# Last transposes in two bank pairs and last output in two column halves, in a fused RWKV-7 and SoLU kernel

## Chip, cores and metric

The kernel runs on one core of a Trainium2 chip. The metric is device time in microseconds (us), the median of several runs. The engines of the core run side by side, each through its own queue in program order, and meet by semaphores: PE (matrix products and transposes), DVE (vector), ACT (scalar and activations), POOL (GpSimd; it also issues DMAs) and SP (SyncE; it issues DMAs only). Products land in PSUM. This kernel treats PSUM as four pairs of banks named A, B, C and h, each 128 partitions by 2 x 512 fp32 values.

## The reference

An RWKV-7 attention over 4 batches, 8 heads, 768 steps and 40 values a head, whose output, as a matrix of 3072 tokens by 320, goes through a SoLU block of width 1024:

```python
for t in range(S):
    y[:, :, t] = np.einsum('bhd,bhde->bhe', rt, state)
    Sa = np.einsum('bhde,bhe->bhd', state, at)
    state_decay = state * wt[:, :, None, :] - np.einsum('bhd,bhe->bhde', Sa, bt)
    state = state_decay + np.einsum('bhd,bhe->bhde', vt, kt)
...
h = x @ w_in
h_max = np.max(h, axis=-1, keepdims=True)
e = np.exp(h - h_max)
sm = e / (np.sum(e, axis=-1, keepdims=True) + 1e-09)
solu = h * sm
mu = np.mean(solu, axis=-1, keepdims=True)
var = np.mean((solu - mu) ** 2, axis=-1, keepdims=True)
ln = (solu - mu) / np.sqrt(var + 1e-06) * g_ln
return (ln @ w_out).astype(np.float32)
```

The gain g_ln and the subtraction of the mean are folded into the output weights (`w2`), and the division by the root of the variance is applied last, row by row (`rs`).

## The kernel before

The work is cut into N = 24 chunks: 12 stretches of 64 time steps for each of two pairs of batches. A chunk is 128 rows (two batches by 64 steps). One loop, `for i in range(-1, N + LAG + 1)` with LAG = 2 (L943), holds a software pipeline. In iteration i the attention works at chunk i (and prepares i + 1 to i + 5), the SoLU block's first product and its softmax work at chunk c = i - 2, and the transposes and the second product work at chunk c - 1 = i - 3. From i = 24 on there is no attention left; i = 25 holds the softmax of chunk 23, the last, and i = 26 only the transposes and output of chunk 23. The order on each engine is the order in which the program emits the instructions.

The steps of the SoLU block, with their lines:

- `hidden` (L741 and on; products recorded at L285, tile `h`): x times w_in, in five pieces of the contraction, into pair h. `left` (L733) issues the loads of xT for it on SP (L739), from the DRAM tile x_dram that `leave` writes by three POOL DMAs (L729 to L731).
- `highest` (L762, DVE, nmax), `exped` (L770, ACT, e), `weighed` (L778, DVE: e becomes h times e, and its mean mu).
- `spreadof` (L781): ACT computes the sum of squares `sq` (L791), whose full-size result is thrown away into a PSUM pair, then `var` (L792); POOL raises it to the power -0.5, `rs` (L793).
- `folded` (L795): sixteen PE transposes (L804) of e, two for each of the eight features (a feature is 128 of the 1024 columns), into one pair, `plnT`. One ACT copy (L809), emitted somewhat later, brings all of it into the SBUF tile lnT.
- `output` (L814): for each of the eight features two products 160 columns wide (`in_parts`, recorded at L285, tile `po`); each shows as two passes in the trace, so a chunk has 32. Then `stored`: ACT multiplies by rs into `osb` (L828) and two DMAs of 64 rows by 320 columns write the output (L831), both on SP except for chunk 23, whose second one goes by ACT's queue. In the steady iterations two of the eight features are held back to the next iteration (the list `rest`); chunk 22's `stored` alone is held back in `late`.

In the last iterations the pairs are used so. `turn` names B and C in alternation as X and Y. The products of `hidden` go to h. The transposes go to h up to chunk 20 and to turn["Y"] for chunks 21 to 23 (`last`, L800). `sq` goes to h, and to A for chunks 22 and 23 (L791). The products `pyo` of `read` (L685) go to A; `summed` (L699, DVE) reads them, and `finish`, what it returns, is `leave`, which makes x and issues the x_dram DMAs. In iteration 26 the order on PE is: the transposes of chunk 23, then chunk 23's products; those of chunk 22 came whole in iteration 25.

Of the kernel before, what the change touches and what calls it, by code (L numbers as in the profile page):

```python
# [9 lines left out]
FP32 = mybir.dt.float32  # L10
# [3 lines left out]
AF = mybir.ActivationFunctionType  # L14
# [3 lines left out]
P = 128  # L18
C = 64
Q = 32  # L20
GRP = 2
AHEAD = 5
LANDS_NEXT = {2: 6, 3: 7, 4: 8, 5: 11, 6: 9, 7: 10, 8: 12}
LAG = 2
EARLY = 10
NK = 5
FIRST = 6
# [26 lines left out]
def kernel(  # L54
# [18 lines left out]
    nc = tc.nc  # L73
    B, H, S, D = r.shape
    DM = H * D
    DFF = moe_w_in.shape[1]
    NCH = S // C
    NPAIR = B // 2
    N = NPAIR * NCH
    NF = DFF // P  # L80
# [5 lines left out]
    two = ctx.enter_context(tc.tile_pool(name="two", bufs=2))  # L86
# [12 lines left out]
    def c_(name):  # L99
        lo, hi = where[name]  # L100
        return cst[:, lo:hi]

    ident, tri = c_("ident"), c_("tri")
# [20 lines left out]
    for x in ex_t:  # L124
# [10 lines left out]
                          in_=c_("eye_hi").unsqueeze(1).to_broadcast([P, 8, Q]))  # L135
# [5 lines left out]
    w2 = const.tile([P, NF, DM], FP32, name="w2")  # L141
# [3 lines left out]
    def pair(tag, name):  # L145
        return psum.tile([P, 2, 512], FP32, tag=tag, name=name)

    turn = dict(X="B", Y="C")
# [119 lines left out]
    def half(p):  # L268
        return slice(C * p, C * p + C)
# [14 lines left out]
    def mm(o, lhsT, rhs, start=True, stop=True):  # L284
        nc.tensor.matmul(o, lhsT=lhsT, rhs=rhs, start=start, stop=stop, skip_group_check=True)  # L285
# [3 lines left out]
    def in_parts(o, lhsT, rhs, start, stop, n=2):  # L289
        width = rhs.shape[-1] // n  # L290
        for x in range(n):
            part = slice(width * x, width * x + width)
            mm(o[:, part], lhsT, rhs[:, part], start and not x, stop)
# [8 lines left out]
    st = [dict() for _ in range(N + 16)]  # L302
    blocks, inverse = {}, {}

    def where_(i):
        return i % NPAIR, i // NPAIR
# [7 lines left out]
    def ok(i):  # L314
        return 0 <= i < N
# [33 lines left out]
    def logged(i):  # L349
        lw = st[i]["lw"] = two.tile([P, DM], FP32, tag="lw", name="lw", bufs=1)  # L350
        nc.scalar.activation(out=lw, in_=st[i]["raw_w"].rearrange("p h d -> p (h d)"), func=AF.Ln)  # L351
# [61 lines left out]
    def decay_turned(i, t=None, y=0):  # L413

        if not ok(i):
            return lambda: None
        ex = st[i]["ex"] = ex_t[i % (AHEAD + 2)]
        t = turned(pair("B", "pei") if t is None else t, y, ei_t[0])
        return lambda: nc.scalar.copy(out=ex[0:W2, :, :, 1:], in_=t)

    def front(i, t=None, y=0):
        if not ok(i):
            return lambda: None
        d = st[i]
        t = turned(pair("C", "pa") if t is None else t, y, d["raw_a"])
        aT = d["aT"] = tokens("aT", AHEAD)
        return lambda: nc.vector.tensor_tensor(out=aT[0:W2], in0=t, in1=d["ex"][0:W2, :, :, 0:C], op=ALU.mult)
# [157 lines left out]
    def attend_r(i, t, y):  # L585
        if not ok(i):
            return lambda: None
        t = turned(t, y, r_t[0])

        def evict():  # L590
            st[i]["rT"] = kept("rT", t)
        return evict
# [179 lines left out]
    def weighed(i):  # L772

        if not ok(i):
            return
        d = st[i]
        d["mu"] = small.tile([P, 1], FP32, tag="mu", name="mu")
        nc.vector.scalar_tensor_tensor(out=d["e"], in0=d["h"], scalar=1.0 / DFF, in1=d["e"], op0=ALU.mult, op1=ALU.mult,  # L778
                                       accum_out=d["mu"])

    def spreadof(i):  # L781

        if not ok(i):
            return
        d = st[i]
        c2 = small.tile([P, 1], FP32, tag="c2", name="c2")
        sq = small.tile([P, 1], FP32, tag="sq", name="sq")
        var = small.tile([P, 1], FP32, tag="var", name="var")
        rs = d["rs"] = small.tile([P, 1], FP32, tag="rs", name="rs")
        nc.scalar.activation(out=c2, in_=d["esum"], func=AF.Square, scale=1e-3 / DFF, bias=guard)  # L790
        nc.scalar.activation(out=pair("A" if i > N - LAG - 1 else "h", "sq").rearrange("p a b -> p (a b)"), in_=d["e"], func=AF.Square, scale=-float(DFF), bias=d["mu"], accum_out=sq)  # L791
        nc.scalar.activation(out=var, in_=sq, func=AF.Identity, scale=1.0 / DFF ** 3, bias=c2)  # L792
        nc.gpsimd.tensor_tensor(out=rs, in0=var, in1=mhalf, op=ALU.pow)  # L793

    def folded(i):  # L795
        if not ok(i):
            return lambda: None
        d = st[i]
        lnT = d["lnT"] = two.tile([P, NF, P], FP32, tag="lnT", name="lnT", bufs=1)
        last = i > N - LAG - 2  # L800
        t = pair(turn["Y"] if last else "h", "plnT")
        for f in range(NF):
            for p in range(2):
                nc.tensor.transpose(out=t[:, p, f * C:f * C + C], in_=d["e"][half(p), f * P:(f + 1) * P],  # L804
                                    identity=ident[half(p), half(p)])

        def evict():
            o, y = lnT.rearrange("q f (p t) -> q p f t", p=2), t.rearrange("q p (f t) -> q p f t", f=NF)
            nc.scalar.copy(out=o, in_=y)  # L809
        return evict  # L810

    late, rest = [], []

    def output(i, t, first=NF):  # L814
        if not ok(i):
            return
        d = st[i]
        bp, ci = where_(i)
        t = t[:, 0:DM]

        def products(lo, hi):
            for f in range(lo, hi):
                in_parts(t, d["lnT"][:, f, :], w2[:, f, :], f == 0, f == NF - 1)
        products(0, first)

        def stored():
            osb = two.tile([P, DM], FP32, tag="osb", name="osb", bufs=1)
            nc.scalar.mul(out=osb, in_=t, mul=d["rs"])  # L828
            for p in range(2):
                queue = nc.scalar if i == N - 1 and p else nc.sync  # L830
                queue.dma_start(out=out.rearrange("(b s) n -> b s n", b=B)[2 * bp + p, ci * C:ci * C + C], in_=osb[half(p)])  # L831
        if first < NF:
            rest.append((lambda: products(first, NF), stored))
        elif i == N - 2:
            late.append(stored)
        else:
            stored()

# [104 lines left out]
    for i in range(-1, N + LAG + 1):  # L943
        j, c = i + AHEAD, i - LAG
# [17 lines left out]
        if i < EARLY - AHEAD:  # L962
            tc_, ta = pair("C", "pa"), pair("A", "pb")
            front_out, r_out = front(j, ta, 0), attend_r(i + 1, ta, 1)
            fold_out = folded(c - 1)
            ei_out, b_out = decay_turned(j + 1, tc_, 0), front_b(j, tc_, 1)
            kv_out = attend_kv(i + 1, pair(turn["X"], "pkv"))
            r_out()
            front_out()
            if i < EARLY - AHEAD:  # L970
                vector(plan[0])
                fold_out()
                b_out()
            else:
                b_out()
                vector(plan[0])
                fold_out()
            s_out = stated(i + 1, pair("A", "pst"), 0) if ok(i + 1) else lambda: None
            for evict in (ei_out, kv_out, s_out):
                evict()  # L980
        else:
            turn.update(zip("XY", ("BC", "CB")[(i - EARLY + AHEAD) % 2]))
            ta = pair("A", "pa")
            front_out, b_out = front(j, ta, 0), front_b(j, ta, 1)
            kv_out = attend_kv(i + 1, pair(turn["Y"], "pkv"))
            front_out()
            kv_out()
            b_out()
            for products, stored in rest:
                products()  # L990
                stored()
            rest.clear()
            vector(plan[0])
            fold_out = folded(c - 1)
            ts = pair("A", "pst")
            s_out = stated(i + 1, ts, 0) if ok(i + 1) else lambda: None
            tc_ = pair(turn["X"], "pb")
            r_out, ei_out = attend_r(i + 1, tc_, 0), decay_turned(j + 1, tc_, 1)
            if i == EARLY - AHEAD and ok(j + 2):
                logged(j + 2)  # L1000
            cum_out = decay_by_halves(j + 2, ts)
            for evict in (r_out, ei_out, fold_out, s_out, *late):
                evict()
            late.clear()
# [65 lines left out]
        finish = summed(i)  # L1070
# [3 lines left out]
            decay(j + 2, pair("C", "pcum")[:, 0])()  # L1074
        tb = pair(turn["X" if i < EARLY - AHEAD else "Y"], "po")
        weighed(c)
        spreadof(c)
        if i >= 0:
            some(Q, (i + 2) // GRP)
# [5 lines left out]
            if odd:  # L1085
                load_keys(j + 3, "k")
                load_keys(j + 5, "w")
        finish()
        vector(plan[5])
        output(c - 1, tb[:, 0], FIRST if EARLY - AHEAD <= i < N - 1 else NF)  # L1090
        if i == -1:
            turn_g(tb[:, 0])
        if i == LAG - 1:
# [33 lines left out]
```

## Time and profile before

| what | value |
|---|---|
| median of 3 runs | 542.85 us (542.31 to 543.46) |
| profiled execution, its own time | 546.59 us |
| its span, first to last instruction | 544.4 us |
| PE busy | 485.0 us, 89% |
| DVE, ACT, POOL busy | 427.4 (79%), 314.4 (58%), 221.0 (41%) us |
| mean granted PE clock | 0.975 |
| HBM read and written | 47.96 and 14.16 MB |

The span is cut by the page into 40 slices of 13.6 us, each digit the busy share in tenths. In the last three slices PE stands at 9, 9 and 6 and DVE at 3, 2 and 0. The stretch that the change touches runs from 501.7 us (the transposes of chunk 20) to the end. In it the trace has the SoLU blocks of chunks 21, 22 and 23, one after the other, each some 9.6 us, the attention of chunk 23 in the first 10 us, and then the last output. Idle time of an engine costs something only where the chain of waits, followed back from the last instruction, goes through it.

### The profile page before, as it was taken

To read this page: it belongs to the slowest core of one execution; us is meant where nothing else is said; L and a number is where in the kernel's file an instruction comes from. 1 tells how busy PE (TensorE), PEld (TensorE's weight loads), DVE (VectorE), ACT (ScalarE), POOL (GpSimd) and SP (SyncE) were. 2 spreads that over 40 slices of the span, in tenths; PEclk is the share of its full clock that TensorE was granted. 3 is DMA by queue.
4 is the path that set the end of the run, shared out by engine and by line. 5 is a ranking of instruction groups with operands and counts; after the bars stand their busy time and mean duration, and the time that the engine had idled before them with its cause. 6 is when DMAs were issued, how large, how long until landed. Compare 5 with 4: busy or idle time off the path is not lost.

```text
span 544.4 us, 28043 instructions
## 1 busy us (share of the span) xinstructions
PE 485.0 (89%) x12029; PEld 397.4 (73%) x12029; DVE 427.4 (79%) x1753; ACT 314.4 (58%) x626; POOL 221.0 (41%) x368
## 2 busy tenths in 40 slices
PE   4634665888999999999999999999999999999996
PEld 3523565756878878878887888788778877787765
DVE  4595998999988987997987979979979798443320
ACT  4733466568467666656665765665556655665333
POOL 4544546244253534536354363545444421211100
PEclk9999975699999999999999999999999999999999
DMA  8998878766455666666684676576563552411210
GB/s 144 160 144 154 191 134 199 159 139 136 74 125 115 114 126 126 138 131 117 132 153 104 115 149 126 114 136 120 113 123 97 108 117 56 104 44 30 54 55 24
DMA packets 198155, 63.95 MB, mean 117 GB/s; under 512 B 170904, under 2 KB 190336, under 8 KB 198032
## 3 DMA queue, kind: packets, MB, share of 16 engines
q1 hardware_dynamic: 185296, 42.22, 42.7%
q0 software_dynamic: 10384, 19.30, 14.7%
q8 instruction: 94, 1.54, 1.2%
q10 hardware_dynamic: 2352, 0.66, 0.7%
q14 instruction: 29, 0.24, 0.2%
HBM read 47.96 MB, written 14.16 MB: 114 GB/s over the span
## 4 chain that ended last, share of the span: by engine, by line
PE 72%; DVE 11%; ACT 7%; DMA 5%; issue 2%; SPq 2%; POOL 0%; ACTq 0%; POOLq 0%; DVEq 0%
PE po L285 19%; PE h L285 18%; PE px L285 6%; PE pyo L285 6%; PE py L285 5%; PE ps L285 3%; PE pu L285 3%; DVE prod L516 2%; DVE uu L519 2%; PE plnT L804 2%; PE pb L400 2%; PE psr L285 2%; DMA raw_w<-in_w_dram 2%; PE pa L400 2%; PE pkv L400 1%
## 5 line engine op out<-in xcount | busy, mean ns | idle before, releaser
L285 PE MATMUL h<-w_in,xT 64*64 64x512 f32 (+1 forms) x1064 | 122.2, 551 | 1.1 <-ACT lnT L809 1.1
L285 PE MATMUL po<-w,lnT 128*128 128x160 f32 x768 | 115.1, 304 | 1.2 <-ACT lnT L809 1.2
L285 PEld LDWEIGHTS po<-w,lnT 128*128 128x128 f32 x768 | 105.4, 190 | 5.8 <-ACT lnT L809 1.3
L519 DVE TENSOR_TENSOR uu<-uu,prod 128x48 f32<-128x48 f32 (+19 forms) x576 | 105.7, 223 | 0.0
L516 DVE TENSOR_TENSOR prod<-blk,uu 128x48 f32<-128x48 f32 (+19 forms) x576 | 102.9, 218 | 1.4
L483 POOL DMA_DIRECT2D nt_dram<-nt x86 | 51.0, 599 | 81.2 <-ACT nt L475 80.0
L793 POOL TENSOR_TENSOR rs<-var,mhalf 128x1 f32<-128x1 f32 x24 | 18.2, 757 | 148.4 <-ACT var L792 148.4
L762 DVE TENSOR_REDUCE nmax<-h 128x1 f32<-128x1024 f32 x24 | 29.3, 1219 | 31.9 <-PE h L285 31.9
L285 PEld LDWEIGHTS h<-w_in,xT 64*64 64x64 f32 x1064 | 38.3, 133 | 19.6 <-issue 14.8
L791 ACT ACTIVATE sq<-e,mu 128x1024 f32<-128x1024 f32 x24 | 26.9, 1119 | 24.2 <-DVE e L778 24.2
L770 ACT ACTIVATE e<-h,nmax 128x1024 f32<-128x1024 f32 x24 | 26.7, 1111 | 21.0 <-DVE nmax L762 21.0
L444 DVE TENSOR_TENSOR lu<-pu,cst 128x512 f32<-128x512 f32 x24 | 16.5, 686 | 25.9 <-PE pu L285 25.6
L311 POOL DMA_DIRECT2D raw_r<-in_r_dram x48 | 33.3, 699 | 0.6 <-issue 0.6
L558 ACT ACTIVATE wy<-py,cst 128x256 f32<-128x256 f32 x24 | 11.4, 474 | 38.1 <-PE py L285 38.1
L508 DVE SCALAR_TENSOR_TENSOR uu<-blk,uu 128x30 f32<-128x30 f32 (+3 forms) x144 | 29.1, 254 | 3.8 <-DMA blk<-nt_dram 3.2
L778 DVE SCALAR_TENSOR_TENSOR e<-h,e 128x1024 f32<-128x1024 f32 x24 | 29.2, 1216 | 3.6 <-ACT e L770 3.4
L393 POOL TENSOR_TENSOR kb<-raw_b,inv 128x320 f32<-128x320 f32 x24 | 21.1, 878 | 26.5 <-DMA raw_b<-in_b_dram 19.1
L617 ACT COPY st<-psr 128x416 f32<-128x416 f32 (+1 forms) x44 | 14.2, 375 | 29.4 <-PE psr L285 29.4
L285 PEld LDWEIGHTS py<-tu,nt 64*64 64x64 f32 x768 | 17.8, 145 | 17.2 <-issue 12.0
L285 PE MATMUL pcum<-lw,cst 128*128 128x160 f32 x48 | 15.3, 465 | 15.9 <-ACT lw L351 15.9
L285 PEld LDWEIGHTS py<-aT,bT 40*64 40x64 f32 x768 | 17.8, 155 | 15.7 <-issue 8.1
L664 ACT ACTIVATE x<-px 128x832 f32<-128x832 f32 x24 | 20.7, 864 | 11.0 <-PE px L285 11.0
(146 smaller groups left out, 1107.1 us busy)
## 6 DMA issues: line engine op xcount, KB each, us to landing
xT<-x_dram SPq DMA_DIRECT2D x48, 160.0 KB
blk<-nt_dram POOLq DMA_DIRECT2D x22, 256.0 KB, 4.1
raw_w<-in_w_dram SPq DMA_DIRECT2D x48, 80.0 KB
a<-in_a_dram SPq DMA_DIRECT2D x48, 80.0 KB
raw_r<-in_r_dram POOLq DMA_DIRECT2D x48, 80.0 KB, 4.3
lv<-in_v_dram SPq DMA_DIRECT2D x48, 80.0 KB
out_dram<-osb SPq DMA_DIRECT2D x47, 80.0 KB
raw_b<-in_b_dram SPq DMA_DIRECT2D x44, 80.0 KB
```

Of the source, the lines that this page charges most:

```text
L285: nc.tensor.matmul(o, lhsT=lhsT, rhs=rhs, start=start, stop=stop, skip_group_check=True)
L311: queue.dma_start(out=x[half(p), :, 0:D], in_=ap[2 * bp + p, :, ci * C:(ci + 1) * C, :].rearrange("h t d -> t h d"))
L393: nc.gpsimd.tensor_tensor(out=kb[:, j:j + H, 0:D], in0=d["raw_" + n], in1=heads(d["inv"]), op=ALU.mult)
L400: nc.tensor.transpose(out=t[0:W2, p, at + C * j:at + C * j + C], in_=x[half(p), 2 * j:2 * j + 2].rearrange("p a b -> p (a b)")[:, skip:ski ...
L483: queue.dma_start(out=blocks[n][e].rearrange("(a x h) s c -> a x s h c", a=GRP, x=2)[at, x], in_=nt[home:home + Q].rearrange("p h j c -> p ...
L508: nc.vector.scalar_tensor_tensor(out=u[:, c, j + 1:Q], in0=nb[:, j, j + 1:Q], scalar=u[:, c, j:j + 1], in1=u[:, c, j + 1:Q], op0=ALU.mult, ...
L516: nc.vector.tensor_tensor(out=ts[-1], in0=nb[:, j:j + 1, j + 1:Q].to_broadcast([P, hi - lo, m]), in1=u[:, lo:hi, j:j + 1].to_broadcast([P, ...
L519: nc.vector.tensor_tensor(out=u[:, lo:hi, j + 1:Q], in0=u[:, lo:hi, j + 1:Q], in1=x, op=ALU.add)
L762: nc.vector.tensor_reduce(out=nmax, in_=d["h"], axis=AX.X, op=ALU.max, negate=True)
L770: nc.scalar.activation(out=e, in_=d["h"], func=AF.Exp, bias=d["nmax"], accum_out=d["esum"])
L778: nc.vector.scalar_tensor_tensor(out=d["e"], in0=d["h"], scalar=1.0 / DFF, in1=d["e"], op0=ALU.mult, op1=ALU.mult, accum_out=d["mu"])
L791: nc.scalar.activation(out=pair("A" if i > N - LAG - 1 else "h", "sq").rearrange("p a b -> p (a b)"), in_=d["e"], func=AF.Square, scale=-f ...
```

## The change

Chunk 20's transposes go to pair A in place of h. In iteration 23 `finish()` is emitted ahead of `spreadof`. One feature of chunk 22's output is held back and emitted behind the transposes of chunk 23; chunk 22's eviction stays in `late`, behind the copies of lnT. Chunk 23's transposes go to two pairs, four features in turn["Y"] and four in A, copied out by DVE and ACT into two tiles. Chunk 23's `sq` goes to h. Its output is computed 160 columns at a time into two pairs, h and turn["Y"], each with an eviction and two stores of 64 rows by 160 columns; the fourth store goes by ACT's queue.

```diff
-        nc.scalar.activation(out=pair("A" if i > N - LAG - 1 else "h", "sq").rearrange("p a b -> p (a b)"), in_=d["e"], func=AF.Square, scale=-float(DFF), bias=d["mu"], accum_out=sq)
+        nc.scalar.activation(out=pair("A" if i == N - 2 else "h", "sq").rearrange("p a b -> p (a b)"), in_=d["e"], func=AF.Square, scale=-float(DFF), bias=d["mu"], accum_out=sq)
...
+        if i == N - 1:
+            return folded_last(d)
         lnT = d["lnT"] = two.tile([P, NF, P], FP32, tag="lnT", name="lnT", bufs=1)
-        last = i > N - LAG - 2
-        t = pair(turn["Y"] if last else "h", "plnT")
+        t = pair("h" if i < N - LAG - 2 else "A" if i == N - LAG - 2 else turn["Y"], "plnT")
...
+    def folded_last(d):
+        n = NF // 2
+        d["lnT"] = (two.tile([P, 2 * n, P], FP32, tag="kvT", name="lnT", bufs=1),
+                    two.tile([P, 2 * n, P], FP32, tag="lnT", name="lnT", bufs=1))
+        ts = pair(turn["Y"], "plnT"), pair("A", "plnT")
+        for f in range(NF):
+            for p in range(2):
+                nc.tensor.transpose(out=ts[f // n][:, p, f % n * C:f % n * C + C],
+                                    in_=d["e"][half(p), f * P:(f + 1) * P], identity=ident[half(p), half(p)])
+
+        def evict():
+            for copy, lnT, t in zip((nc.vector.tensor_copy, nc.scalar.copy), d["lnT"], ts):
+                copy(out=lnT[:, 0:n].rearrange("q f (p t) -> q p f t", p=2),
+                     in_=t[:, :, 0:n * C].rearrange("q p (f t) -> q p f t", f=n))
+        return evict
+
+    def output_last(i):
+        d = st[i]
+        bp, ci = where_(i)
+        n, width = NF // 2, DM // 2
+        for x, tag in enumerate(("h", turn["Y"])):
+            cols = slice(width * x, width * x + width)
+            t = pair(tag, "po")[:, 0, 0:width]
+            for f in range(NF):
+                mm(t, d["lnT"][f // n][:, f % n, :], w2[:, f, cols], f == 0, f == NF - 1)
+            osb = two.tile([P, 4 * P], FP32, tag=("s", "x")[x], name="osb", bufs=1)[:, 0:width]
+            nc.scalar.mul(out=osb, in_=t, mul=d["rs"])
+            for p in range(2):
+                queue = nc.scalar if x and p else nc.sync
+                queue.dma_start(out=out.rearrange("(b s) n -> b s n", b=B)[2 * bp + p, ci * C:ci * C + C, cols], in_=osb[half(p)])
...
-                queue = nc.scalar if i == N - 1 and p else nc.sync
-                queue.dma_start(out=out.rearrange("(b s) n -> b s n", b=B)[2 * bp + p, ci * C:ci * C + C], in_=osb[half(p)])
+                nc.sync.dma_start(out=out.rearrange("(b s) n -> b s n", b=B)[2 * bp + p, ci * C:ci * C + C], in_=osb[half(p)])
...
-        elif i == N - 2:
-            late.append(stored)
...
+            if i == N + LAG:
+                fold_out = folded(c - 1)
             for products, stored in rest:
                 products()
-                stored()
+                if i == N + LAG:
+                    late.append(stored)
+                else:
+                    stored()
             rest.clear()
             vector(plan[0])
-            fold_out = folded(c - 1)
+            if i < N + LAG:
+                fold_out = folded(c - 1)
...
         weighed(c)
+        if i == N - 1:
+            finish()
         spreadof(c)
...
-        finish()
+        if i != N - 1:
+            finish()
         vector(plan[5])
-        output(c - 1, tb[:, 0], FIRST if EARLY - AHEAD <= i < N - 1 else NF)
+        if i == N + LAG:
+            output_last(c - 1)
+        else:
+            output(c - 1, tb[:, 0], NF - 1 if i == N + LAG - 1 else FIRST if EARLY - AHEAD <= i < N - 1 else NF)
```

## The prediction

> **What bounds the kernel now.** First the page's busy shares: PE 89%, DVE 79%, ACT 58%, and the granted clock 0.975. Only the end of the program is edited: the order of instructions on every engine is the same up to chunk 20's transposes, so I read the chain of waits there. Its columns are start and length in us, then what ran.
>
> ```profile
> 497.25 4.54 PE po L285 x32
> 501.80 0.66 PE plnT L804 x16
> 502.45 0.02 issue
> 502.48 1.02 ACT lnT L809
> 503.50 0.04 issue
> 503.54 1.09 PE h L285 x8
> ...
> 525.04 4.53 PE h L285 x40
> 529.57 0.02 issue
> 529.60 1.24 DVE nmax L762
> ...
> 533.36 1.25 ACT sq L791 x2
> 534.61 0.02 issue
> 534.63 0.14 ACT var L792
> 534.77 0.06 issue
> 534.83 1.00 ACT lnT L809
> 535.84 0.04 issue
> 535.88 4.63 PE po L285 x32
> ...
> 540.66 0.53 ACT osb L828
> ```
>
> From 502 on PE sets the end, except in two places. At 502.45 it has finished the transposes of chunk 20 and stands until ACT has copied them out at 503.50, because chunk 21's first product goes to the pair h that still holds them. At 529.57 the last softmax begins (nmax, exp, e, sq, var, then the copy lnT, one after the other), and chunk 23's products start at 535.88. The waits of the same stretch price both stops (total, times, longest, in us):
>
> ```profile
> PE po L285 <- ACT lnT L809: 1.2, 1, 1.2
> PE h L285 <- ACT lnT L809: 1.1, 1, 1.1
> ```
>
> After the last product come one eviction, two stores side by side, and SyncE's wait for them:
>
> ```profile
> 541.22 0.54 ACTq L831 DMA_DIRECT2D out_dram<-osb  x1
> ```
>
> ```profile
> SPq L1122 <- DMA out_dram<-osb: 1.4, 1, 1.4
> ```
>
> **The change, part by part.** Times are on the clock of before; the first part moves all later ones alike.
>
> *Chunk 20's transposes in pair A.* The h products of chunk 21 no longer wait for L809. They could start when the sixteen transposes end, 502.45, as they do in the next chunk, where plnT runs 514.75 to 515.39 and h starts at 515.39. Gain 503.54 - 502.45 = 1.09. What else they need is there: sq of chunk 20, which also writes h, ends at 501.11 (its accumulator read, 500.92 + 0.19), and xT of chunk 21 was issued at 488.65; the loads issued at 507.34 and 519.14 had their last packets at 510.56 and 522.09, some 3 us later. Pair A is free: its last reader, the sum tot, began at 497.32 and took 1.09. The new wait falls on pyo of chunk 23, which takes A after the copy ends at 503.50; PE comes to it at 506.88 - 1.09 = 505.79, with 2.3 us to spare. Behind it on PE are the rest of h and everything after.
> Does the lead last? Each later step (h, nmax, exp, e, transposes) hangs on PE's own products, so they move together. The one input that does not move is xT of chunk 22, landed at 510.56 and needed at 515.33 - 1.09 = 514.24. I take the whole 1.09; the ends are 0 and 1.12.
>
> *finish() ahead of spreadof at i = 23.* On POOL the three x_dram issues (L729 to L731: 0.69 + 0.58 + 0.54 = 1.8 us) now stand before rs of chunk 21, which waited for var. They start when x is ready (L725: 513.24 + 0.76 = 514.00) and not at 515.63. ACT and DVE order are unchanged. xT of chunk 23 then lands 1.6 us earlier relative to PE; its last packet came at 522.09 and it was needed at 524.97, and the whole chain moves together, so 2.9 us of room grow and are worth nothing. SP keeps its order, so its next issue, the store of chunk 20, waits as before for ACT. rs of chunk 21 ends near 514.00 + 1.8 + 0.56 = 516.4 and its reader, osb of chunk 21, ran at 525.19: hidden by 8.8 us. Cost 0; without that cover 0.8 (516.4 against 515.63).
>
> *One feature of chunk 22 behind the last transposes.* Chunk 22's 16 products (32 passes) run 529.43 to 533.97, 4.54 / 32 = 0.142 us a pass; e of chunk 23 is ready at 533.32. With 28 passes first, PE is free at 529.43 + 28 x 0.142 = 533.40, and after a wake-up of about 0.05 (lnT's copy ends 535.82, the weight load starts 535.88) the transposes start at 533.45, not 533.97. They take 0.64, to 534.09, and the four passes left 0.57, to 534.66.
>
> *Two bank pairs, DVE and ACT.* The eighth transpose ends at 533.45 + 0.32, with 0.07 of drain (h issues end 529.50, its chain piece 529.57); DVE starts at 533.87. A DVE copy of 128x512 is not in the trace; the 104x512 copy bT L440 took 0.68, the 128x512 product L444 0.69. So it ends at 534.55, and PE may read it at 534.61: just before PE is done with chunk 22. ACT waits for the last feature of chunk 22 (a signal stands there in the built program, none at the sixteenth transpose), which costs nothing, since var holds ACT until 534.83; behind that copy on ACT stand chunk 22's osb and the last two. Its half takes 0.59 (rT L410, 104x512), to 535.42; PE needs it after eight passes, 534.66 + 1.14 = 535.80. So chunk 23's products start at 534.66 and not at 535.88: gain 1.22. Ends: 0.95 if the DVE copy costs as much as ACT's whole one (1.00), 1.28 if no wake-up costs anything. Chunk 22's osb slips behind the copy, its rs is ready at 525.98, and its store ends far ahead of the last one.
>
> *The last output by 160 columns.* The same 32 passes of the same width run in another order: 0. The first half's osb and stores lie under the second half's 2.27 us of products: products done at 536.93, osb to 537.4, SP's two issues to 538.5; chunk 22's two, ahead of them on SP, end near 537.1, and the last store comes at 539.9, so nothing on SP holds it. Of the last osb, 160 columns go: copies of 416 and 96 columns took 505 and 244 ns (L617), so 0.82 ns a column, 0.13 (ends 0 and 0.33, the latter from 196 ns for 8 columns, L243). PE's end now stands as a wait on the activation itself, where 540.51 to 540.66 held a separate wait: 0.05, ends 0 and 0.11.
> The stores halve. The last two were issued at 541.21; the packets, 1280 bytes each, ran 542.34 to 543.13 one transfer behind the other, and completion was seen at 543.49. A 1280-byte packet took 55 ns, a 512-byte one 27 (xT), so 640 bytes should take about 32: 0.79 x (1 - 32/55) = 0.33 at best, 0 if issue sets the pace. I take 0.25, since the two transfers followed without a gap. The Trainium skill, "DMA: Bandwidth & Descriptors", section "Anatomy of one DMA", gives about 2.0 us fixed for a transfer and the rest by bytes at 436 GB/s, fitted on another issue path; by that the 80 KB less are worth an estimated 0.19, and the sum would be 0.06 smaller. The 2.28 us from issue to completion, of which packets are 0.79, agree with a mostly fixed price.
> A loss stands behind it. SyncE ends with a row of semaphore waits, about 0.062 apart (541.78, 541.84, 541.90, ...). In before the last stores hold lanes six and seven, so one wait followed the one that ended at 543.49; now they hold lanes zero and one at the row's head, and seven follow: +6 x 0.062 = 0.37 (ends 0 and 0.37).
>
> **Sum.** -1.09 - 1.22 - 0.13 - 0.05 - 0.25 + 0.37 = -2.37. On the profiled execution: span 544.4 to 542.0; its own time, 546.59, would be 544.2. The runs' median is 542.85, 3.74 below that profiled run; the tail's waits are the same in both, so 542.85 - 2.37 = 540.5. Unknown terms at their ends, the first held at 1.09: -1.67 to -3.14, so 539.7 to 541.2 for the likeliest case.
>
> **Rivals.**
> 1. The two halves are not really apart: DVE's copy is released only with the last signal, behind chunk 22's feature. It would start at 534.66 + 0.10, end at 535.44, and products start at 535.50: 0.84 lost, total -1.53, 541.3. For it: ACT's half is released just so. Against: the eighth transpose carries a signal of its own in the built program. 8%.
> 2. The 1.09 is given back: pyo of chunk 23 or xT of chunk 22 is what PE then waits for. Total -1.28, 541.6. For: two waits are added at A. Against: 2.3 and 3.7 us of room. 6%.
> 3. Little moves, because what the first 500 us vary by from run to run covers it, or both stops return elsewhere: about 542.4, between 0 and -1.09. For: the three runs span 1.15 us. Against: not one instruction there is reordered. 8%.
> 4. Slower: a PE without its two rests loses clock. The page's row of granted clock shows that this can happen:
>
> ```profile
> PEclk9999975699999999999999999999999999999999
> ```
>
> Slices six to eight stand at 7, 5 and 6. PE's 37 us from 503 to 540 at a share x take 37 (1/x - 1) more; against the 2.37 that decides from x = 0.94, and at 0.88 costs 5.0, so 545.5. Against: 32 slices of nine follow, at PE busy 9, and the rests are 1.1 and 1.2 us. 3%.
>
> **How the numbers follow.** Forecast 75%, the rivals 8, 6, 8 and 3. The predicted time is 540.5. A measurement of this kernel can tell about 0.2%, 1.09 us, from no change. Rivals 1 and most of 2 count as faster: 0.75 + 0.08 + 0.04 = 0.87. Same 0.10, slower 0.03. The range takes in the likeliest's 539.7 to 541.2, rivals 1 and 2, and 0.3 of run-to-run scatter below: 539.4 to 541.9. That leaves out rivals 3 and 4 and little else.
>
> **What would show it.** In the changed profile: h of chunk 21 starts with no wait for lnT; pyo of chunk 23 doesn't wait; the last transposes start within 0.1 us of e's end; DVE's lnT copy takes about 0.68 and ends as the last four passes of chunk 22 do; PE then runs on without a gap until the last osb of some 0.40; from the last issue to the end of the span it is 3.2 us plus or minus 0.3. It is wrong if PE waits over 0.3 us for either half of lnT, if a new wait shows between 503 and 529, or if the last stores' packets take as long as before.

## The result and the profile after

| | before | changed |
|---|---|---|
| median | 543.02 us (11 runs, 542.31 to 544.17) | 540.13 us (11 runs, 538.11 to 542.55) |
| profiled execution: time, span | 546.59, 544.4 | 538.5, 536.7 |
| chunk 20's transposes begin at | 501.72 | 496.35 |
| from there to the end of the span (the tail) | 42.72 | 40.37 |

The ratio of the times is 0.9941, 95% interval 0.9924 to 0.9957: the kernel became 2.3 to 4.1 us faster, against 2.37 forecast. The two profiles differ by 7.7 us, and most of that is not the change. The changed kernel's profile is already 5.37 us ahead where the first changed instruction stands. A tail counted from that point takes this out: 42.72 - 40.37 = 2.35. A run's time is also longer than its span, by 2.14 us in the profiled execution of before and by 1.78 in that of the changed kernel; this difference is taken up at the end of the section on the prediction.

The chain of waits of the changed kernel, start and length in us:

```profile
491.88 4.54 PE po L285 x32
496.42 0.64 PE plnT L805 x16
497.07 1.02 PE h L285 x8
...
522.96 4.00 PE po L285 x28
526.96 0.64 PE plnT L820 x16
527.60 5.23 PE po L285 x36
532.83 0.02 issue
532.86 0.39 ACT osb L839
```

Both stops of before, at 502.45 and at 529.57 on its clock, are gone. After chunk 20's transposes PE goes straight to h, and the last softmax (nmax, exp, e, sq, var) is no longer on the chain: it lies beside the 28 passes of chunk 22. From there to the last product the chain stays on PE: 28 passes, 16 transposes and 36 passes, with one short wait of 0.1 us for DVE's copy inside the 36. The timeline shows how the two copies meet it (start, length, engine, what; in brackets the idle time before and what ended it):

```profile
526.89 0.57 PEld L820 LDWEIGHTS plnT<-cst,e 64*128 64x128 f32 x16 [0.17 <-DVE e L778]
527.40 0.69 DVE L825 COPY lnT<-plnT 128x512 f32<-128x512 f32 x1 [0.61 <-PE plnT L820]
527.53 5.05 PEld L285 LDWEIGHTS po<-w,lnT 128*128 128x128 f32 x36
...
528.38 0.58 ACT L825 COPY lnT<-plnT 128x512 f32<-128x512 f32 x1
```

DVE's copy starts while PE is still at the second eight transposes, so it has its own signal. It ends at 528.09, and chunk 23's products begin at 528.20. ACT's copy ends at 528.96, ahead of their need after eight passes. SyncE's wait for the last stores, which was 1.4 us in before:

```profile
SPq L1163 <- DMA out_dram<-osb: 1.6, 1, 1.6
```

It is longer although the stores are half as large, since it now begins at the head of SyncE's closing row of semaphore waits.

### The profile page after: what moved, and what is told of

Same layout as the page of the kernel before. It is cut to its first block, busy times and chain, and to the rows that moved or that the text cites. A ratio compares the mean times of both kernels' runs of the same rounds, so it can differ in the third digit from the quotient of the medians.

```text
span 536.7 us, 28054 instructions
## 1 busy us (share of the span) xinstructions
PE 480.9 (90%) x12029; PEld 393.6 (73%) x12029; DVE 427.2 (80%) x1754; ACT 314.3 (59%) x627; POOL 222.1 (41%) x368
## 4 chain that ended last, share of the span: by engine, by line
PE 72%; DVE 9%; ACT 6%; DMA 5%; SPq 4%; issue 2%; POOL 1%; ACTq 0%; DVEq 0%; POOLq 0%
PE po L285 20%; PE h L285 18%; PE px L285 5%; PE pyo L285 5%; PE py L285 5%; PE ps L285 3%; PE pu L285 3%; DMA uu_dram<-uu 2%; PE plnT L805 2%; SPq L311 2%; PE pb L400 2%; PE psr L285 2%; PE pa L400 2%; DVE prod L516 2%; DVE uu L519 2%
## 5 line engine op out<-in xcount | busy, mean ns | idle before, releaser
L516 DVE TENSOR_TENSOR prod<-blk,uu 128x48 f32<-128x48 f32 (+19 forms) x576 | 104.5, 221 | 1.4
```

The source lines that it names most:

```text
L516: nc.vector.tensor_tensor(out=ts[-1], in0=nb[:, j:j + 1, j + 1:Q].to_broadcast([P, hi - lo, m]), in1=u[:, lo:hi, j:j + 1].to_broadcast([P, ...
```

## The experiments

All tails are counted from the first weight load of chunk 20's transposes, which every kernel has at the same place in its order of instructions.

**e0_before_again**: the kernel before, without an edit.

> The kernel before, unaltered, profiled once more. The tail is measured from the first weight load of chunk 20's transposes to the end of the span: 42.73 us in the first profile of before (501.72 to 544.45), 40.37 in the changed kernel (496.35 to 536.72). Theory (the whole effect lies in the tail, and the 5.37 us by which the changed kernel's profile is ahead when the tail begins are scatter between executions): tail 42.7 within 0.1, while the start of the tail moves by some us from 501.7. Rival (the changed kernel also gains before the tail): the tail starts near 501.7 again, within 1 us.

Measured: tail 42.73, begun at 501.03. The tail repeats to 0.01 us, as both theories have it; the start moved by 0.7 only, which is the rival's number. One more execution was too few. Over all profiles of this study the tail begins at 501.72 and 501.03 (before), 498.56 (e1), and at 496.35, 500.60, 500.26, 498.10, 501.88, 502.99, 498.50, 496.93 and 497.63 (the changed kernel, e2 to e9). The same instructions in the same order stand ahead of that point in all twelve. Kernels with the changed end lie on both sides of before's, 6.6 us apart among themselves. The runs were made on several chips (e0 to e3 on chip 4, e4 to e7 on chip 6, e8 and e9 on chip 10), but the chip alone does not explain it: e4 to e7 begin 4.9 us apart on one chip, and before's own spans in 17 runs on that chip go from 540.1 to 547.4. So the 5.37 between the first two profiles is within the scatter of executions.

**e1_pair_a_only**: before, with chunk 20's transposes in A.

```diff
-        t = pair(turn["Y"] if last else "h", "plnT")
+        t = pair(turn["Y"] if last else "A" if i == N - LAG - 2 else "h", "plnT")
```

> The kernel before with one part alone: chunk 20's transposes go to pair A. Theory: PE no longer stands before chunk 21's first product, and the lead lasts to the end: tail 42.73 - 1.17 = 41.56, products of chunk 21 start within 0.1 us of the transposes' end, last copy of lnT and last products as in before. Rival (the lead is given back at xT of chunk 22 or 23 or at pyo of chunk 23): tail 42.7 and a new wait between 503 and 529 on the clock of before.

Measured: tail 41.55, a gain of 1.17. The end of its chain is that of before, piece by piece:

```profile
530.50 1.00 ACT lnT L809
531.50 0.04 issue
531.54 4.63 PE po L285 x32
```

**e2_back_to_h**: the changed kernel without that part.

```diff
-        t = pair("h" if i < N - LAG - 2 else "A" if i == N - LAG - 2 else turn["Y"], "plnT")
+        t = pair("h" if i < N - LAG - 1 else turn["Y"], "plnT")
```

> The changed kernel with chunk 20's transposes back in pair h. Theory: the stop of 1.1 us before chunk 21's products returns and nothing else changes: tail 40.37 + 1.17 = 41.54. Rival (the two gains are not additive, the last chunk hides part of it): tail below 41.3.

Measured: tail 41.53, a loss of 1.16, and the old wait is back in the list of waits (total, times, longest):

```profile
PE h L285 <- ACT lnT L810: 1.1, 1, 1.1
```

Done alone and undone alone, the part is worth the same 1.17. The two gains add, and the lead is not given back.

**e3_no_feature_back**: all of chunk 22's products ahead of the last transposes.

```diff
+        elif i == N - 2:
+            late.append(stored)
...
-            output(c - 1, tb[:, 0], NF - 1 if i == N + LAG - 1 else FIRST if EARLY - AHEAD <= i < N - 1 else NF)
+            output(c - 1, tb[:, 0], FIRST if EARLY - AHEAD <= i < N - 1 else NF)
```

> The changed kernel with all eight features of chunk 22's output ahead of the last transposes, as in before. Theory: the transposes start 0.54 us later (when PE is done with chunk 22), DVE's copy too, and PE stands about 0.9 us from the transposes' end to the end of that copy, since no products are left to fill the time: last products start 0.45 to 0.6 later, tail 40.8 to 41.0. Rival (DVE's half is what counts and the held feature hides nothing that matters): tail within 0.15 of 40.37.

Measured: tail 40.91, a loss of 0.54. Its timeline has PE idle where the changed kernel has four passes:

```profile
531.34 0.71 PE L820 MATMUL plnT<-cst,e 64*128 64x64 f32 x16
531.85 0.69 DVE L825 COPY lnT<-plnT 128x512 f32<-128x512 f32 x1 [1.16 <-PE plnT L820]
...
532.69 4.58 PE L285 MATMUL po<-w,lnT 128*128 128x160 f32 x32 [0.63 <-DVE lnT L825]
```

The wait for DVE is 0.63, not the 0.9 expected. The loss comes out as forecast because it is the lateness of the transposes that is paid, 0.54.

**e4_act_copies_both**: ACT copies both halves.

```diff
-            for copy, lnT, t in zip((nc.vector.tensor_copy, nc.scalar.copy), d["lnT"], ts):
+            for copy, lnT, t in zip((nc.scalar.copy, nc.scalar.copy), d["lnT"], ts):
```

> The changed kernel with both halves of the last lnT copied by ACT, none by DVE. Theory: ACT can begin only behind var, so the first half ends where ACT's half ended (1.44 us after the DVE copy began plus 0.1) and the last products start 0.8 to 0.9 us later: tail 41.2 to 41.3. Rival (what helps is the split into two pairs, not the second engine): tail within 0.3 of 40.37.

Measured: tail 41.06, a loss of 0.69, less than either number I had for the theory and well more than the rival's.

```profile
530.04 1.05 ACT L825 COPY lnT<-plnT 128x512 f32<-128x512 f32 x2
...
530.65 4.37 PEld L285 LDWEIGHTS po<-w,lnT 128*128 128x128 f32 x32 [0.81 <-ACT lnT L825]
```

The first half begins 0.20 after var does (529.84). In the changed kernel ACT's half began 0.29 after it (528.09 to 528.38), for it also waits for chunk 22's last feature, and I had carried that wait over to a copy that doesn't have it. Within the tail, chunk 23's products begin 0.71 later than in the changed kernel (32.56 against 31.85). So of the 1.13 us by which they begin earlier in the changed kernel than in before, DVE's copy is worth 0.71. The 0.42 left belongs to the split alone: ACT's first copy begins 0.20 after var, as before's whole copy did, and takes 0.57 in place of 0.99. The held feature brings nothing here, since ACT is not free until 530.04 and the transposes are done at 529.27; it needs DVE's copy to be worth its 0.54.

**e5_whole_output**: the last output in one piece of 320 columns.

```diff
...
-        for x, tag in enumerate(("h", turn["Y"])):
...
-                mm(t, d["lnT"][f // n][:, f % n, :], w2[:, f, cols], f == 0, f == NF - 1)
+        t = pair("h", "po")[:, 0, 0:DM]
+        for f in range(NF):
+            in_parts(t, d["lnT"][f // n][:, f % n, :], w2[:, f, :], f == 0, f == NF - 1)
...
```

> The changed kernel with the last output whole: 320 columns into pair h, one eviction, two stores. Theory: the last eviction is 0.14 longer, the time from the last issue to the last store's completion 0.16 longer, but the last stores hold lanes six and seven again, so SyncE's closing waits are 0.37 shorter: tail 40.37 - 0.07 = 40.30 within 0.1. Rival (the column halves are a gain of their own, the closing waits cost nothing): tail 40.67.

Measured: tail 40.36, the same as the changed kernel's 40.37. From the last weight load to the eviction it takes 0.53 us (0.47 in halves), the eviction 0.527 (0.394), issue to completion 2.28 (2.12), completion to the end 0.96 (1.32). The first three are 0.35 longer and the last is 0.36 shorter. In this kernel the column halves were worth nothing: what they save before the last completion, the closing waits take back.

**e6_rs_first**: finish() behind spreadof again at iteration 23.

```diff
         weighed(c)
-        if i == N - 1:
-            finish()
         spreadof(c)
...
-        if i != N - 1:
-            finish()
+        finish()
```

> The changed kernel with finish() behind spreadof at iteration 23, as in before. Theory: xT of chunk 23 has room either way, so the tail stays 40.37 within 0.1, and only the three x_dram issues are 1.6 us later. Rival (with PE 1.17 us ahead the load is needed): PE waits for xT before chunk 23's products and the tail is longer by 0.3 or more.

Measured: tail 40.36. The x_dram issues come 1.3 us later within the tail (515.72 against 507.74, begun at 502.99 and 496.35), the load of xT behind them 1.6 us later (519.24 and 511.04), and nobody waits.

**e7_lanes**: chunk 22's two stores by POOL, which has nothing else to do by then; this shifts which semaphores (lanes, taken in turn) the last stores signal.

```diff
-                nc.sync.dma_start(out=out.rearrange("(b s) n -> b s n", b=B)[2 * bp + p, ci * C:ci * C + C], in_=osb[half(p)])
+                (nc.gpsimd if i == N - 2 else nc.sync).dma_start(out=out.rearrange("(b s) n -> b s n", b=B)[2 * bp + p, ci * C:ci * C + C], in_=osb[half(p)])
```

> The changed kernel with chunk 22's two stores issued by POOL instead of SP, so that chunk 23's four stores hold lanes four to seven. Theory: one closing wait of SyncE follows the last completion instead of seven, 6 x 0.062 us less: tail 40.0, and a time 0.4 us below the changed kernel's 540.1. Rival (the closing waits overlap something else that sets the end): tail 40.4.

Measured: tail 39.98, completion to the end 0.95 in place of 1.32. SyncE's wait, 1.6 in the changed kernel, is

```profile
SPq L1163 <- DMA out_dram<-osb: 1.2, 1, 1.2
```

since the first seven waits of the row now run while the stores are under way. The time is 543.06 against 545.2 for before in the same runs, ratio 0.9955 (0.9928 to 0.9982). On that chip all times stood higher, before's too (545.2), so 543.06 is not to be set beside 540.13; the ratio cannot tell this version from the changed kernel, the tail can: 0.39 us.

**e8_dve_last**: e7_lanes, with the very last eviction by DVE.

```diff
-            nc.scalar.mul(out=osb, in_=t, mul=d["rs"])
+            if x:
+                nc.vector.tensor_scalar(out=osb, in0=t, scalar1=d["rs"], scalar2=None, op0=ALU.mult)
+            else:
+                nc.scalar.mul(out=osb, in_=t, mul=d["rs"])
```

> e7_lanes with the very last eviction by DVE instead of ACT. DVE's 1024 columns take 1.22 us (nmax) and 512 take 0.69 (lnT), so about 1.04 ns a column and 0.32 for 160, against ACT's 0.39. Theory (only that eviction is on the path there): tail 39.98 - 0.07 = 39.91. Rival (DVE starts later from PE's signal, or the stores issued by two queues wait longer for DVE's): tail 39.98 or more. Against before in the same runs: 42.73 - 39.91 = 2.82 us, a ratio near 0.9948.

Measured: tail 40.04, 0.06 worse than e7_lanes; the theory fell.

```profile
533.49 0.38 DVE L840 TENSOR_SCALAR osb<-po,rs 128x160 f32<-128x160 f32 x1 [4.83 <-PE po L285]
```

DVE's 160 columns took 0.38 us, not 0.32: the line through 512 and 1024 columns of other operations doesn't hold for this one. It also began 0.395 us after the start of PE's last pass, where ACT began 0.336 after it in e7_lanes. Ratio to before 0.9942 (0.9921 to 0.9964), against 0.9948 expected.

**e9_after_again**: the changed kernel, without an edit.

> The changed kernel once more, unaltered, timed against before in five rounds. Theory (the tail is the whole effect): tail 40.37, and a difference of 2.36 us between the times, a ratio near 0.9957. Rival (the changed kernel also gains before the tail, as its first median, 2.89 us below before, might suggest): a ratio at or below 0.9945.

Measured: tail 40.36; 539.99 against 543.02, ratio 0.9947 (0.9924 to 0.9970). The tail repeats. The interval holds 0.9957, the tail's 2.36 us alone, and values below 0.9945 as well, so these five rounds do not tell the theory from the rival. A third possibility was in neither: a gain outside the span (see the end of the next section).

## Why the prediction was right

The forecast was 540.5, the median 540.13; the tail moved by 2.35 where the sum said 2.37. The mechanism was right in the two large terms and in the closing waits. That the sum is right to 0.02 is partly luck: four terms are off by 0.07 to 0.09, two each way. Term by term, all from the two profiles, counted within the tail:

| step of the prediction | forecast | measured |
|---|---|---|
| h of chunk 21 without the wait | -1.09 | -1.18 |
| last products earlier | -1.22 | -1.13 |
| PE's end to the last eviction | -0.05 | -0.12 |
| last eviction, 160 columns | -0.13 | -0.13 |
| last issue to completion | -0.25 | -0.16 |
| completion to the end | +0.37 | +0.36 |

*Chunk 20's pair.* Right, and e1 and e2 each show it alone. The size was 0.08 short: the start of a product that waits for nothing overlaps the last transpose's drain (in the changed kernel's timeline the transposes end at 497.07 and h starts at 497.00), and I had counted from the chain's piece, where the drain is over.

*The held feature.* Right: the transposes came 0.54 earlier within the tail (forecast 0.52), and e3 loses that 0.54.

*The two copies.* The mechanism was right and the size 0.09 too large. From the transposes' start to chunk 23's products it took 1.32, not 1.21, since DVE's copy began 0.51 after the first weight load and not 0.42, and so became what the products wait for, by 0.11; I had it a hair ahead of PE. The copy itself, 0.69, was as priced. e4 shows what DVE brings: 0.71.

*The end.* The eviction and the closing waits were right. The way from PE's end to the eviction became 0.125 shorter, just beyond the 0.11 given as that term's end; e5, with the output whole, keeps half of this (0.53, against 0.60 in before and 0.47 in the changed kernel), and what makes up the two halves was not shown. The stores were mis-sized: each transfer's 640-byte packets took 32 ns, as estimated, but the whole row still took 0.62 us (534.405 to 535.026) where before had 0.79 and 0.54 was forecast. So half the bytes saved a fifth of the packets' time, not the third that 0.25 stands for. The 55 ns for 1280 bytes was the median of ACT's store alone; the packets of SyncE's took 88, so the ratio 32 to 55 was not that of the row. The estimate of 0.19 from the Trainium skill's fit ("DMA: Bandwidth & Descriptors", section "Anatomy of one DMA") was nearer to the 0.16 measured than my 0.25. From the last issue to the end of the span it took 3.44, inside the stated 3.2 plus or minus 0.3; the sum's own terms make it 3.36 there (3.24 in before, less 0.25, plus 0.37).

*What cost nothing.* finish() ahead of spreadof (e6) and chunk 22's later eviction: no wait for either in the trace.

*The rivals.* The first (one signal for both halves) falls with DVE's start ahead of chunk 22's last feature. The second (the 1.09 given back) falls with e1, e2 and the list of waits, which has no new stop. The third (little moves) falls with the interval, 2.3 to 4.1 us, although the starts of the tail do scatter by more than the change is worth. The fourth (less clock) falls with the granted clock of the changed kernel, which averages 1.00 over the tail, as it does in before, although PE no longer rests there. Its row:

```profile
PEclk9999975899999999999999999999999999999999
```

It stands at nine in every slice from the ninth on.

*What the prediction left out.* The medians differ by 2.89 and the tails by 2.35. Part of the rest lies outside the span. A run's time exceeds its span by 2.11 to 2.21 us in the 37 runs of before that were timed beside the experiments, and by 1.74 to 1.83 in the 19 runs of the changed kernel. The prediction carried this part over from before unchanged, that is, it put a gain of about 0.37 us at nothing, and that is the size by which the median came out below 540.5; that the two agree so closely proves nothing, given the scatter. The gain goes with DVE's copy of lnT: the kernels whose last work on DVE is that copy (e2, e3, e5, e6, e7 and the changed kernel) have 1.74 to 1.83, those without it (before, e1, and e4 in its one run) 2.10 to 2.21, and e8, where DVE also has the last eviction, 1.82 to 2.08. Why was not shown. What then stays open is 2.89 - 2.35 - 0.37 = 0.2 us, and 3.03 - 2.36 - 0.38 = 0.3 in e9. It lies within the intervals and within the scatter of the tail's start, and no instruction ahead of the tail was moved; but that it is only scatter was not shown.

## What to carry to other kernels

Where only the end of a program is edited, count both profiles from the last instruction that they share: here that turned a difference of 7.7 us with 5.4 of scatter in it into six terms, each of which could be read to 0.02 us. Then look at what lies outside the span as well: here that moved by 0.37, as much as the closing waits. Where a transposed tile and the next accumulation share a bank pair, the bottleneck engine stops for as long as the copy out of that pair takes (1.0 us here), and a pair that is idle at that point takes the stop away. At the very end look past the last completion: the closing waits stand in a fixed order, and which semaphores the last stores signal cost as much here (0.36) as halving the last piece brought (0.35), so that e7_lanes, with both, has the shortest tail.

## What was not expected of the hardware

- The tail is repeatable to 0.02 us (42.72, 42.73; 40.37, 40.36; and chunk 21's first product begins 1.82 into the tail in the three profiles with chunk 20's transposes in h and 0.64 in the nine with them in A), while the 500 us ahead of it, with the same instructions, end anywhere from 496.35 to 502.99 in twelve profiles. The difference does not arise in one place: the profiles are 2.4 us apart at chunk 0's transposes (127.0 to 129.4), 4.0 at chunk 2's and 7.1 at chunk 10's.
- The granted clock differs between executions, in slices four to nine; the latest start of all (e6, 502.99) has the row below. Yet its mean does not order the starts: e3 has 0.984 and begins the tail at 500.26, e4 has 0.965 and begins it at 498.10. What sets the scatter was not tried.

```profile
PEclk9998575689999999999999999999999999999999
```

- Two stores issued side by side by SyncE and ACT move their packets almost one store after the other: in the changed kernel (640-byte packets) SyncE's run from 534.40 to 534.74 and ACT's from 534.69 to 535.03, in before (1280 bytes) 542.34 to 542.86 and 542.68 to 543.13. Each store's packets spread over 0.34 us at 640 bytes and 0.45 to 0.52 at 1280, so halving the size does not halve the row.
